# Memory attention and a maxout FFN on one core: output tiles in two pieces, and a new order of issue

## The chip, the cores and the metric

The kernel runs on one core of a Trainium2 chip. Its engines are TensorE (PE, matrix products into PSUM), VectorE (DVE), ScalarE (ACT) and GpSimd (POOL); SyncE (SP) issues transfers. Transfers run on 16 DMA engines. The metric is the device time of one execution in microseconds, the median of several runs; lower is better. PSUM has 8 banks of 512 fp32 columns on 128 partitions.

## The reference

Attention over 32 memory slots for 8 batches, 8 heads, 576 positions, head width 64, followed by an FFN whose hidden layer is the largest of three products:

```python
a = exp(phi - max_s phi);  a = a / (sum_s a + 1e-9)      # over positions s
k_m = einsum('bhsm,bhsd->bhmd', a, k)
v_m = einsum('bhsm,bhsd->bhmd', a, v)
attn = softmax(q @ k_m.T / 8) @ v_m                       # (b, h, s, d)
x = attn.transpose(0, 2, 1, 3).reshape(4608, 512)
h = max(max(x @ w1, x @ w2), x @ w3)                      # 512 -> 768
out = h @ w_out                                           # 768 -> 512, fp32
```

All inputs and the output are fp32 in HBM; the kernel's matrix products are in bf16.

## The kernel before, in words

**Staging.** q, k, v and phi come in whole batches. POOL issues these loads, and the weights; they convert to bf16 on the way, phi excepted. SP issues the first phi and the outputs. k and v of a batch lie in one of two buffers `kvo`; from batch 2 on POOL packs them into one of two buffers `kvr` (`pack`, L102), one copy for each of k and v, so that one product gives k_m, v_m and the softmax's denominators together. In batches 0 and 1 they are taken straight from `kvo`, in two parts. `ph` and `qq` have two buffers each. `wait_for` (L127) is a one-element copy on POOL that waits for half of k of batch 0, so that the loads issued behind it start later.

**One batch.** `att_exp` (ACT) gives e; `att_kv` (PE, L256) k_m and v_m; `att_kv_norm` (DVE) divides; `att_kv_t` transposes on PE and copies out. `att_q` (DVE) shuffles q; `att_score` (PE, L340) gives scores and ACT their exponentials; `att_t`, `att_sum`, `att_rec` (DVE), `att_mul` (POOL, L416) and `att_back` (DVE) make the probabilities `attn`, in two halves g = 0 and 1. Batch 0 takes its sums by PE instead (`ones_sum`, `ones_rec`, `ones_mul`).

**The FFN without the attention's last product.** v_m is multiplied into the weights: `fold` (PE, L447) gives wp = v_m times (w1-w3, w2-w3), and wp3 = v_m times (w3 times w_out), for 32 slots a head. `w_diff` (DVE) makes the differences in place; batch 0 folds w1, w2 and -w3 before they are made, in the column ranges of `FIRST`. `w3_t` and `w3_o` make w3 times w_out once. Then `ffn1` (PE, L473) is four products of 288 columns from attn and wp; w = 0 (even n) ends in a relu into h1, w = 1 (odd n) in a maximum with h1 on DVE into hT. So h - x w3 is what hT holds. `ffn2` (PE, L504 to L522) is one output tile of 128 rows: six products of hT with w_out and two of attn with wp3, summed in one PSUM bank, copied out, and stored by SP. Batches go in pairs of 1152 rows; tile t = 4 of an odd batch straddles the two batches of a pair (four half-width products). `ffn2_last` does the very last tile in two halves.

**The order.** Nothing reorders: each engine runs its instructions in the order in which a string of words at the end (L602 to L625) issues them. A word is a letter, a number and a batch: `F10@2` is `ffn1` n = 10 of batch 2. The letters are in `issue` (L568):

- L loads a batch (0 phi, 1 k, 2 v, 3 q), H half of k (even) or v (odd) of batch 0 (0, 1 the first half, 2, 3 the second); Y the weights (2 w3, 0 w1, 1 w2, 3 w_out); G the wait on POOL; r packs (0 k, 1 v); I identity and constants
- E exp of phi, B `att_kv`, N `att_kv_norm`, K `att_kv_t`, Q `att_q`, S `att_score`, a, s, c, m, X the softmax's steps, M and R the sums of batch 0, V `w_diff`
- D fold (3 is wp3), F `ffn1`, T `ffn2`, W and O the product of w3 and w_out, Z that many warm-up products of zeros

A "!" gives the copy out of PSUM to the other of ACT and DVE than the table `EVAC` says. A second string (`banks`, L145) gives the PSUM bank of each group in the order of issue; `one_bank` takes one, `two_banks` a pair. `fts` keeps the order in which a batch's hT tiles were made, and `ffn2` sums in this order.

Of the kernel before, what the change touches and what calls it, by code (L numbers as in the profile page):

```python
# [15 lines left out]
def kernel(  # L16
# [583 lines left out]


    for w in """  # L602
        E@0 H0@0 H2@0 L3@0 Z25@0 B0@0 I@0 N0@0 Z2@0 K0@0! Q0@0 Q1@0 Z9@0 S@0 Z2@0 M0@0 M1@0
        R0@0 Y2@0 G0@0 R1@0 W0@0 Y3@0 W1@0 W2@0 Z6@0 O1@0 H3@0 O3@0 O2@0 H1@0 X1@0 B1@0 X0@0 N1@0
        K1@0 O0@0 Y0@0 D1@0! D0@0! D3@0 F8@0 F10@0 F2@0 V0@0 F6@0 F0@0! Y1@0 D2@0 D4@0 F4@0
        L0@1 V1@0 F1@0 E@1 F3@0 L1@1 F5@0 F9@0 F7@0 L3@1 F11@0 B0@1 T3@0 N0@1 K0@1! L2@1 Q1@1
        L2@2 L1@2 Q0@1 L0@2 V2@0 T0@0! L3@2 S@1 T1@0 a0@1 s0@1 c0@1 m0@1 B1@1 N1@1 a1@1 L1@3
        K1@1 s1@1 D0@1 D1@1! D2@1 c1@1 m1@1 X0@1 L3@3 r1@2 X1@1 T2@0! L2@3 F6@1 F10@1 F7@1 F2@1
        F3@1 F4@1 F0@1 r0@2 E@2 F5@1 F1@1 F11@1 L0@3 L0@4 F8@1 L2@4 F9@1 B@2 D3@1 N@2 Q1@2
        T0@1! K@2 T2@1! r0@3 Q0@2 S@2 a0@2 a1@2 s1@2 c1@2 m1@2 T4@1! D1@2! s0@2 D2@2 c0@2 m0@2  # L610
        X1@2 D0@2 T3@1 Q0@3 L3@4 X0@2 Q1@3 T1@1 F0@2 F4@2 F8@2 F6@2 F9@2 E@3 F7@2 r1@3 F5@2
        F10@2 F1@2 B@3 L1@4 D3@2 N@3 L0@5 F2@2 F11@2 E@4 F3@2 L1@5 K@3 r1@4 L2@5 T2@2! S@3 T3@2
        a0@3 s0@3 c0@3 m0@3 D0@3 D2@3 a1@3 s1@3 c1@3 X0@3 D1@3! Q0@4 m1@3 T1@2 L3@5 L2@6 T0@2!
        X1@3 F10@3 r0@4 F2@3 F4@3 E@5 Q1@4 r0@5 F5@3 F3@3 L1@6 F8@3 B@4 N@4 D3@3 F9@3 F6@3
        F11@3 L0@6 K@4 F0@3 F7@3 F1@3 S@4 a0@4 T4@3! s0@4 a1@4 D0@4 c0@4 s1@4 r1@5 c1@4 D3@4
        m0@4 X0@4 Q0@5 T0@3! D1@4! D2@4 B@5 T3@3 m1@4 X1@4 L0@7 F10@4 Q1@5 N@5 F8@4 K@5 F6@4
        F9@4 S@5 F7@4 L3@6 F2@4 F4@4 a0@5 L1@7 a1@5 F0@4 s0@5 r1@6 F3@4 D0@5 r0@6 s1@5 c1@5 E@6
        D3@5 m1@5 c0@5 F1@4 T1@3 L2@7 F11@4 L3@7 E@7 F5@4 m0@5 B@6 D1@5! D2@5 X1@5 N@6 T2@3!
        X0@5 F6@5 F8@5 Q0@6 Q1@6 K@6 F4@5 F9@5 S@6 F7@5 r0@7 a0@6 F2@5 a1@6 s0@6 c0@6 F0@5
        F10@5 m0@6 F1@5 s1@6 c1@6 F11@5 F5@5 T0@4! F3@5 X0@6 T2@4! r1@7 D0@6 D1@6! Q0@7 B@7  # L620
        m1@6 N@7 X1@6 T2@5! K@7 T3@4 Q1@7 S@7 a0@7 F2@6 s0@7 a1@7 s1@7 c1@7 m1@7 c0@7 F4@6
        T4@5! D3@6 D2@7 D0@7! T0@5! D3@7 D2@6 X1@7 m0@7 D1@7! T1@4 X0@7 F6@7 F3@6 T1@5 F4@7
        F8@7 F0@7 F5@6 F10@6 F7@7 F9@7 F10@7 F5@7 F0@6 F11@7 F6@6 F1@7 F7@6 F2@7 F8@6 F11@6
        F9@6 F1@6 F3@7 T0@6! T0@7! T3@5 T2@7! T2@6! T1@6 T1@7 T3@6 T4@7! T3@7
    """.split():  # L625
# [32 lines left out]
```

## Time and profile before

| | |
|---|---|
| median of 3 runs | 165.57 us (165.14 to 166.01) |
| profiled execution, device time | 165.42 us |
| its span, first to last instruction | 163.7 us |
| last matmul starts its group at | 159.56 us |
| bytes moved by DMA | 31.77 MB, 194 GB/s over the span |
| output stores | 35 of 256 KB, two of 128 KB |

The span is what the profile's rows are measured in; the device time has 1.7 us around it. Lines of the timeline read: start, length, engine, line, operation, output<-input, number merged, and in brackets the idle time before it with what ended it. In the list of windows a row is the stretch, its length, then for PE, weight loads, DVE, ACT and POOL the busy time and the number of instructions, then the granted clock, the share of the DMA engines (over 1 where packets overlap) and GB/s. Lines of the chain are start, length and what ran. Ends of matmuls are modelled, so neighbouring groups overlap a little in these rows.

### The profile page before, as it was taken

What the parts mean: (1) busy time and instruction counts of PE and PEld (TensorE: products, weight loads), DVE (VectorE), ACT (ScalarE), POOL (GpSimd) and SP (SyncE); (2) the same over time, 40 slices, a digit from 0 to 9 for tenths busy, and PEclk for the clock granted to TensorE, in tenths of its full rate; (3) what the DMA queues carried; (4) which work ended last, traced back from release to release, by engine and by line L of the source; (5) the groups of instructions that cost most, each with busy time, mean ns of one, the idle gap of its engine ahead of it and who ended that gap; (6) DMA issues with size and microseconds to landing.
All of it is one profiled execution on the core that took longest, in us unless ns stands there. A gap on an engine that the chain in (4) does not pass through costs nothing.

```text
span 163.7 us, 4819 instructions
## 1 busy us (share of the span) xinstructions
PE 153.0 (93%) x2060; PEld 85.5 (52%) x2080; DVE 90.4 (55%) x181; ACT 100.5 (61%) x151; POOL 69.7 (43%) x72
## 2 busy tenths in 40 slices
PE   7987798999898999999999999999999999999990
PEld 2442444664376436753673575576553467744450
DVE  2023703898837765759399759879749228810000
ACT  4205335935496488778885989994658976323320
POOL 7275215100698276838939976755403200000000
PEclk9999999999999999999999999999999999999999
DMA  5999999999999999999999999997313230014333
GB/s 155 156 207 200 197 210 213 277 208 208 259 307 241 209 257 364 277 216 286 258 265 206 233 351 266 175 235 157 130 70 125 73 128 0 0 68 180 141 128 130
DMA packets 21974, 31.77 MB, mean 194 GB/s; under 512 B 1216, under 2 KB 16576, under 8 KB 21952
## 3 DMA queue, kind: packets, MB, share of 16 engines
q0 software_dynamic: 16080, 21.43, 68.7%
q1 hardware_dynamic: 5728, 9.90, 17.2%
q8 instruction: 16, 0.26, 0.6%
q10 hardware_dynamic: 144, 0.13, 0.2%
q14 instruction: 6, 0.05, 0.1%
HBM read 39.32 MB, written 9.44 MB: 298 GB/s over the span
## 4 chain that ended last, share of the span: by engine, by line
PE 65%; DMA 28%; POOL 2%; issue 2%; ACT 1%; POOLq 0%; ACTq 0%
PE psum L504 25%; PE psum L473 22%; DMA ph<-in_phi_dram 15%; DMA w_sb<-in_moe_w_dram 9%; PE psum L513 7%; DMA kvo<-in_k_dram 4%; PE psum L447 4%; PE psum L256 3%; PE psum L340 1%; POOL kvo L97 1%; PE psum L522 1%; PE psum L545 1%; ACT e L236 1%; PE psum L305 1%; POOL wo_sb L123 0%
## 5 line engine op out<-in xcount | busy, mean ns | idle before, releaser
L504 PE MATMUL psum<-wo_sb,hT 128*128 128x512 bf16 x193 | 49.7, 380 | 1.4 <-issue 0.6
L473 PE MATMUL psum<-attn,wp 128*128 128x288 bf16 x384 | 50.5, 286 | 0.1
L486 DVE TENSOR_TENSOR hT<-psum,h 128x576 bf16<-128x576 f32 x48 | 34.2, 749 | 18.2 <-PE psum L473 12.0
L473 PEld LDWEIGHTS <-wp 128*128 128x128 bf16 x384 | 36.7, 98 | 13.2 <-issue 1.9
L179 ACT COPY ot<-psum 128x512 f32<-128x512 f32 x35 | 20.7, 591 | 32.1 <-PE psum L513 25.2
L504 PEld LDWEIGHTS <-hT 128*128 128x128 bf16 x210 | 19.2, 98 | 24.1 <-issue 4.3
L103 POOL COPY kvr<-kvo 128x2304 bf16<-128x2304 bf16 x12 | 25.4, 2114 | 14.3 <-DMA kvo<-in_k_dram 7.9
L179 ACT CAST wp<-psum 128x1024 bf16<-128x1024 f32 (+1 forms) x31 | 29.3, 996 | 3.0 <-PE psum L447 2.1
L177 ACT ACTIVATE h<-psum 128x576 bf16<-128x576 f32 x47 | 28.4, 659 | 3.2 <-PE psum L473 3.1
L416 POOL TENSOR_TENSOR t<-t,sm 128x576 bf16<-128x576 bf16 x14 | 16.1, 1157 | 25.2 <-DVE sm L411 25.1
L513 PE MATMUL psum<-wp,attn 128*128 128x512 bf16 x62 | 18.4, 379 | 0.0
L166 PE MATMUL psum<-warm 128*128 128x512 bf16 x42 | 12.4, 450 | 1.4 <-DVE warm L135 1.2
L320 DVE STREAM_TRANSPOSE qT<-qq 128x576 f32<-128x576 f32 x16 | 11.7, 747 | 1.5 <-DMA qq<-in_q_dram 1.5
L349 ACT ACTIVATE e<-psum 128x576 bf16<-128x576 f32 x16 | 9.6, 652 | 3.8 <-PE psum L340 3.8
L236 ACT ACTIVATE e<-ph 128x1152 bf16<-128x1152 f32 (+1 forms) x9 | 9.6, 1065 | 2.6 <-DMA ph<-in_phi_dram 2.4
L402 DVE TENSOR_REDUCE sm<-t 128x18 f32<-128x576 bf16 x14 | 10.3, 738 | 0.2
L97 POOL DMA_DIRECT2D kvo<-in_v_dram x9 | 6.7, 747 | 7.2 <-PE psum L256 4.1
L513 PEld LDWEIGHTS <-attn 128*128 128x128 bf16 x62 | 6.1, 98 | 7.1
L394 DVE STREAM_TRANSPOSE t<-e 128x288 f32<-128x288 f32 x14 | 6.3, 464 | 6.2 <-ACT e L349 6.1
L562 DVE COPY ot<-psum 128x256 f32<-128x256 f32 x1 | 0.4, 425 | 15.4 <-PE psum L553 15.4
L256 PEld LDWEIGHTS <-e 64*32 64x32 bf16 x720 | 6.9, 90 | 3.4 <-issue 2.0
L166 PEld LDWEIGHTS <-warm 128*128 128x128 bf16 x44 | 4.6, 111 | 7.4 <-issue 3.5
(58 smaller groups left out, 116.4 us busy)
## 6 DMA issues: line engine op xcount, KB each, us to landing
out_dram<-ot SPq DMA_DIRECT2D x35, 256.0 KB, 5.5
qq<-in_q_dram POOLq DMA_DIRECT2D x8, 576.0 KB, 12.6
ph<-in_phi_dram POOLq DMA_DIRECT2D x7, 576.0 KB, 15.1
kvo<-in_k_dram POOLq DMA_DIRECT2D x7, 576.0 KB, 13.9
kvo<-in_v_dram POOLq DMA_DIRECT2D x7, 576.0 KB, 16.6
w_sb<-in_moe_w_dram POOLq DMA_DIRECT2D x3, 768.0 KB, 15.0
wo_sb<-in_moe_w_out_dram POOLq DMA_DIRECT2D x1, 768.0 KB, 10.7
ph<-in_phi_dram SPq DMA_DIRECT2D x2, 288.0 KB, 2.9
```

Of the source, the lines that this page charges most:

```text
L103: nc.gpsimd.tensor_copy(out=kvrs[b % 2][:, :, :, D * i : D * (i + 1)], in_=kvos[b % 2][:, 1 - i])
L166: nc.tensor.matmul(po[:, 0:BANK], lhsT=warm[:, 0:P], rhs=warm, start=True, stop=True)
L177: nc.scalar.activation(out=out_, in_=in_, func=AF.Relu)
L179: nc.scalar.copy(out=out_, in_=in_)
L236: nc.scalar.activation(out=s["e"][:, js], in_=loaded[b]["ph"][:, js], func=AF.Exp)
L256: nc.tensor.matmul(kvp[M * j : M * (j + 1), a, 0:nd], lhsT=s["e"][r, j, c, :], rhs={None: lambda: kvr[r, j, c, 0:nd], 0: lambda: k_and_one ...
L320: nc.vector.transpose(out=s["qT"][:, j].rearrange("p j c r e -> p (j c r e)").bitcast(FP32), in_=loaded[b]["q"][:, j].rearrange("p j c d - ...
L416: nc.gpsimd.tensor_tensor(out=t, in0=t, in1=s["sm", g].unsqueeze(2).to_broadcast([P, S // HP, R, 2]), op=ALU.mult,)
L473: nc.tensor.matmul(acc[:, h, 0:SH], lhsT=wps[b][:, g, w * DF + ft * P : w * DF + (ft + 1) * P], rhs=attn[:, g, c0 : c0 + SH], start=(g == ...
L486: nc.vector.tensor_tensor(out=hT[:, ft, (b % 2) * S : (b % 2 + 1) * S].rearrange("p (h n) -> p h n", h=2), in0=a, in1=s["h1", ft], op=ALU.max,
L504: nc.tensor.matmul(po, lhsT=hT[:, fc, c0 : c0 + P], rhs=wo_sb[:, fc, :], start=(n == 0), stop=False,)
L513: nc.tensor.matmul(po, lhsT=attn[:, g, c0 : c0 + P], rhs=wp3s[b][:, g, :], start=False, stop=(g == NG - 1),)
```

## The change

- A new word P is `ffn2_head`: the first three of the six hT products of an output tile, into a bank of its own that is held. The word T of the same tile later takes this bank and does the remaining three and the two with wp3. Tiles without a P are whole as before.
- Tile t = 4 does its products with wp3 first and those with hT after.
- `w_diff` works on the ranges of `FIRST`, one instruction a word: V0, V1, V2 and V4 in place of V0, V1 (two instructions) and V2.
- The strings of order and banks are new from start to end: q of batch 0 is loaded first, then the second half of k and the first; the identity is made behind POOL's wait; phi and q of batch 3 are loaded ahead of v and k of batch 3; packs, folds, `ffn1` and tiles stand elsewhere; more copies out of PSUM have a "!".

```diff
--- before.py
+++ after.py
@@ -41,6 +41,7 @@
     FT = DF // P
     SH = S // 2
     BANK = 512
+    HEAD = 3
 
     const = ctx.enter_context(tc.tile_pool(name="const", bufs=1))
     inp = ctx.enter_context(tc.tile_pool(name="inp", bufs=2))
@@ -145,9 +146,9 @@
     banks = iter(
         "".join(
             """
-            00224460026701101401264026402640264026452063420643064206420642064562074206742064
-            20642064201640264102640264026402640264072406247026402640264024602406520462046204
-            62704267402640264124602416420642064206420642067676767670
+            30303012464064726746246024026420642064744074644020426024604260427012442067406420
+            46240642014264621046620642064206425602062672020724042064024602402656056042064202
+            4062452654260620162404204624026420462406240340607336334
             """.split()
         )
     )
@@ -214,16 +215,13 @@
 
     def w_diff(n):
 
-        c, end = n * BANK, (n + 1) * BANK
-        while c < end:
-            e = min(end, (c // DF + 1) * DF)
-            nc.vector.tensor_tensor(
-                out=w12[:, :, c:e],
-                in0=w12[:, :, c:e],
-                in1=w_sb[:, :, 2, c % DF : c % DF + e - c],
-                op=ALU.subtract,
-            )
-            c = e
+        lo, end = FIRST[n]
+        nc.vector.tensor_tensor(
+            out=w12[:, :, lo:end],
+            in0=w12[:, :, lo:end],
+            in1=w_sb[:, :, 2, lo % DF : lo % DF + end - lo],
+            op=ALU.subtract,
+        )
 
     ln = const.tile([P, S], FP32, name="ln")
     ONES = {(0, 0), (0, 1)}
@@ -492,15 +490,15 @@
 
     osts = {}
 
-    def ffn2(b, t, swap):
-
-
-        hT, attn = hts[b // 2], attns[b // 2]
-        c0 = S - HP if t == 4 else (b % 2) * (S + HP) + t * P
-        if b == B - 1 and t == 3:
-            return ffn2_last(b, c0)
-        po = one_bank()
-        for n, fc in enumerate(fts[b]):
+    heads = {}
+
+    def ffn2_head(b, t):
+
+        hT = hts[b // 2]
+        c0 = (b % 2) * (S + HP) + t * P
+        po = heads[b, t] = one_bank()
+        for n in range(HEAD):
+            fc = fts[b][n]
             nc.tensor.matmul(
                 po,
                 lhsT=hT[:, fc, c0 : c0 + P],
@@ -508,8 +506,38 @@
                 start=(n == 0),
                 stop=False,
             )
-        for g in range(NG):
-            if t < 4:
+
+    def ffn2(b, t, swap):
+
+
+        hT, attn = hts[b // 2], attns[b // 2]
+        c0 = S - HP if t == 4 else (b % 2) * (S + HP) + t * P
+        if b == B - 1 and t == 3:
+            return ffn2_last(b, c0)
+        po = heads[b, t] if (b, t) in heads else one_bank()
+
+        if t == 4:
+            for g in range(NG):
+                for u in range(2):
+                    nc.tensor.matmul(
+                        po[HP * u : HP * (u + 1)],
+                        lhsT=attn[:, g, c0 + HP * u : c0 + HP * (u + 1)],
+                        rhs=wp3s[b - 1 + u][:, g, :],
+                        start=(g == 0),
+                        stop=False,
+                        tile_position=(0, HP * u),
+                    )
+        for n in range(HEAD if (b, t) in heads else 0, FT):
+            fc = fts[b][n]
+            nc.tensor.matmul(
+                po,
+                lhsT=hT[:, fc, c0 : c0 + P],
+                rhs=wo_sb[:, fc, :],
+                start=(n == 0 and t < 4),
+                stop=(n == FT - 1 and t == 4),
+            )
+        if t < 4:
+            for g in range(NG):
                 nc.tensor.matmul(
                     po,
                     lhsT=attn[:, g, c0 : c0 + P],
@@ -517,16 +545,6 @@
                     start=False,
                     stop=(g == NG - 1),
                 )
-            else:
-                for u in range(2):
-                    nc.tensor.matmul(
-                        po[HP * u : HP * (u + 1)],
-                        lhsT=attn[:, g, c0 + HP * u : c0 + HP * (u + 1)],
-                        rhs=wp3s[b - 1 + u][:, g, :],
-                        start=False,
-                        stop=(g == NG - 1),
-                        tile_position=(0, HP * u),
-                    )
         ot = opool.tile([P, DM], FP32, name="ot")
         r0 = (b // 2) * 2 * S + c0
         rows = out[r0 : r0 + P, :]
@@ -590,6 +608,7 @@
             "R": lambda: ones_rec(b, i),
             "D": lambda: fold(b, i, swap),
             "F": lambda: ffn1(b, i, swap),
+            "P": lambda: ffn2_head(b, i),
             "T": lambda: ffn2(b, i, swap),
             "W": lambda: w3_t(i, swap),
             "O": lambda: w3_o(i, swap),
@@ -600,28 +619,30 @@
 
 
     for w in """
-        E@0 H0@0 H2@0 L3@0 Z25@0 B0@0 I@0 N0@0 Z2@0 K0@0! Q0@0 Q1@0 Z9@0 S@0 Z2@0 M0@0 M1@0
-        R0@0 Y2@0 G0@0 R1@0 W0@0 Y3@0 W1@0 W2@0 Z6@0 O1@0 H3@0 O3@0 O2@0 H1@0 X1@0 B1@0 X0@0 N1@0
-        K1@0 O0@0 Y0@0 D1@0! D0@0! D3@0 F8@0 F10@0 F2@0 V0@0 F6@0 F0@0! Y1@0 D2@0 D4@0 F4@0
-        L0@1 V1@0 F1@0 E@1 F3@0 L1@1 F5@0 F9@0 F7@0 L3@1 F11@0 B0@1 T3@0 N0@1 K0@1! L2@1 Q1@1
-        L2@2 L1@2 Q0@1 L0@2 V2@0 T0@0! L3@2 S@1 T1@0 a0@1 s0@1 c0@1 m0@1 B1@1 N1@1 a1@1 L1@3
-        K1@1 s1@1 D0@1 D1@1! D2@1 c1@1 m1@1 X0@1 L3@3 r1@2 X1@1 T2@0! L2@3 F6@1 F10@1 F7@1 F2@1
-        F3@1 F4@1 F0@1 r0@2 E@2 F5@1 F1@1 F11@1 L0@3 L0@4 F8@1 L2@4 F9@1 B@2 D3@1 N@2 Q1@2
-        T0@1! K@2 T2@1! r0@3 Q0@2 S@2 a0@2 a1@2 s1@2 c1@2 m1@2 T4@1! D1@2! s0@2 D2@2 c0@2 m0@2
-        X1@2 D0@2 T3@1 Q0@3 L3@4 X0@2 Q1@3 T1@1 F0@2 F4@2 F8@2 F6@2 F9@2 E@3 F7@2 r1@3 F5@2
-        F10@2 F1@2 B@3 L1@4 D3@2 N@3 L0@5 F2@2 F11@2 E@4 F3@2 L1@5 K@3 r1@4 L2@5 T2@2! S@3 T3@2
-        a0@3 s0@3 c0@3 m0@3 D0@3 D2@3 a1@3 s1@3 c1@3 X0@3 D1@3! Q0@4 m1@3 T1@2 L3@5 L2@6 T0@2!
-        X1@3 F10@3 r0@4 F2@3 F4@3 E@5 Q1@4 r0@5 F5@3 F3@3 L1@6 F8@3 B@4 N@4 D3@3 F9@3 F6@3
-        F11@3 L0@6 K@4 F0@3 F7@3 F1@3 S@4 a0@4 T4@3! s0@4 a1@4 D0@4 c0@4 s1@4 r1@5 c1@4 D3@4
-        m0@4 X0@4 Q0@5 T0@3! D1@4! D2@4 B@5 T3@3 m1@4 X1@4 L0@7 F10@4 Q1@5 N@5 F8@4 K@5 F6@4
-        F9@4 S@5 F7@4 L3@6 F2@4 F4@4 a0@5 L1@7 a1@5 F0@4 s0@5 r1@6 F3@4 D0@5 r0@6 s1@5 c1@5 E@6
-        D3@5 m1@5 c0@5 F1@4 T1@3 L2@7 F11@4 L3@7 E@7 F5@4 m0@5 B@6 D1@5! D2@5 X1@5 N@6 T2@3!
-        X0@5 F6@5 F8@5 Q0@6 Q1@6 K@6 F4@5 F9@5 S@6 F7@5 r0@7 a0@6 F2@5 a1@6 s0@6 c0@6 F0@5
-        F10@5 m0@6 F1@5 s1@6 c1@6 F11@5 F5@5 T0@4! F3@5 X0@6 T2@4! r1@7 D0@6 D1@6! Q0@7 B@7
-        m1@6 N@7 X1@6 T2@5! K@7 T3@4 Q1@7 S@7 a0@7 F2@6 s0@7 a1@7 s1@7 c1@7 m1@7 c0@7 F4@6
-        T4@5! D3@6 D2@7 D0@7! T0@5! D3@7 D2@6 X1@7 m0@7 D1@7! T1@4 X0@7 F6@7 F3@6 T1@5 F4@7
-        F8@7 F0@7 F5@6 F10@6 F7@7 F9@7 F10@7 F5@7 F0@6 F11@7 F6@6 F1@7 F7@6 F2@7 F8@6 F11@6
-        F9@6 F1@6 F3@7 T0@6! T0@7! T3@5 T2@7! T2@6! T1@6 T1@7 T3@6 T4@7! T3@7
+        L3@0 H2@0 E@0 H0@0 Z36@0 B0@0 Y2@0 G0@0 Y3@0 I@0 Q1@0 N0@0 Q0@0 Z3@0 K0@0! Z6@0 W2@0
+        W1@0 W0@0 S@0 M0@0 Z3@0 O0@0! R0@0 H3@0 M1@0 O3@0 H1@0 B1@0 R1@0 N1@0 X1@0 X0@0 O2@0
+        K1@0! Y0@0 O1@0 D1@0! V1@0 D0@0! D3@0 F8@0! Y1@0 V0@0 F10@0 F0@0 F2@0 F6@0! D2@0 L0@1
+        L1@1 D4@0 V4@0 F4@0 F3@0 F1@0 F9@0 L3@1 L2@1 L2@2 F5@0 L1@2 F11@0 E@1 F7@0 L0@2 L3@2
+        L0@3 P3@0 B0@1 N0@1 Q0@1 T1@0 K0@1! Q1@1 T3@0! S@1 V2@0 a0@1 P2@0 s0@1 B1@1 N1@1 c0@1
+        P0@0 L3@3 a1@1 m0@1 s1@1 K1@1! c1@1 X0@1 T2@0! D0@1! D1@1! m1@1 D2@1 L2@3 r1@2 X1@1
+        T0@0! F0@1 F10@1! F8@1 F2@1 r0@2 F1@1 F11@1 F4@1 F6@1! F9@1 E@2 F5@1 F3@1 P2@1 F7@1 B@2
+        D3@1 N@2 P0@1 P3@1 K@2! L1@3 T3@1 Q0@2 Q1@2 S@2 a1@2 T2@1! E@3 L2@4 a0@2 L0@4 L1@4 s0@2
+        c0@2 s1@2 c1@2 m0@2 Q1@3 m1@2 L3@4 r1@3 X0@2 r0@3 T0@1! D1@2 L2@5 X1@2 r1@4 D0@2 D2@2
+        T4@1! T1@1! F6@2 F2@2! F7@2 Q0@3 F4@2 F10@2 F3@2 F8@2 F5@2 F9@2 F0@2 F11@2 B@3 N@3 L0@5
+        D3@2 E@4 F1@2 P2@2 K@3 P1@2 S@3 a0@3 T1@2! T2@2! a1@3 s0@3 s1@3 c1@3 L1@5 r0@4 D1@3!
+        c0@3 D3@3 Q0@4 m0@3 D2@3 P3@2 P0@2 B@4 D0@3 L3@5 Q1@4 X0@3 m1@3 T3@2! X1@3 r1@5 T0@2!
+        F6@3 F2@3 F0@3 N@4 F8@3 L0@6 F1@3 F10@3 F7@3 E@5 K@4 F9@3 F3@3 F4@3 F11@3 P0@3 F5@3
+        P1@3 L1@6 S@4 r0@5 L3@6 T4@3! a0@4 s0@4 L2@6 B@5 D1@4! a1@4 s1@4 N@5 c1@4 D2@4 Q0@5
+        T1@3 m1@4 Q1@5 c0@4 m0@4 K@5 X1@4 P2@3 L0@7 T0@3! S@5 L1@7 X0@4 a0@5 T2@3! r0@6 F8@4
+        s0@5 L3@7 a1@5 F10@4 P3@3 s1@5 c1@5 c0@5 D3@4! L2@7 D0@4 D1@5! m0@5 T3@3 F9@4 F4@4!
+        m1@5 F0@4 F5@4 X0@5 F2@4 F6@4 X1@5 F3@4 E@6 F7@4 r1@6 F1@4 F10@5 r0@7 F11@4 P2@4 Q0@6
+        B@6 D0@5! D2@5 T0@4! N@6 F6@5! E@7 Q1@6 Q1@7 F0@5 K@6 T2@4! F2@5! F8@5 F7@5 F3@5 F9@5
+        P3@4 F1@5 F4@5 Q0@7 r1@7 F11@5 T3@4! S@6 B@7 N@7 D3@5 F5@5 P2@5 K@7! T2@5! a0@6 S@7
+        P1@4 a0@7 P3@5 a1@7 D1@7! s0@6 s0@7 D2@7 c0@6 D3@7 a1@6 s1@6 m0@6 s1@7 T3@5 c0@7 T1@4!
+        X0@6 c1@7 m0@7 X0@7 c1@6 D3@6! m1@7 m1@6 D0@7 T1@5 T0@5 D1@6! X1@6 D0@6! X1@7 D2@6
+        T4@5! F4@7 F2@6 F4@6! F6@6 F7@6 F0@7 F3@6 F5@7 F8@7 F5@6 F8@6 F1@7 F6@7! F10@6 F10@7
+        F9@7 F11@6 F11@7 F0@6! P0@7 F9@6 F2@7 P2@6 F1@6 F3@7 P1@7 T2@6! F7@7 T4@7! T2@7 T1@7
+        T1@6 T0@6! T3@6! T0@7! T3@7
     """.split():
         n, b = w.rstrip("!").split("@")
         issue(int(b), n, w.endswith("!"))
```

## The prediction

> **What bounds the kernel now.** I read the page's slices first, then the windows, TensorE's own timeline, and last POOL's timeline, because POOL issues every load after the first.
>
> ```profile
> span 163.7 us, 4819 instructions
> PE 153.0 (93%) x2060; PEld 85.5 (52%) x2080; DVE 90.4 (55%) x181; ACT 100.5 (61%) x151; POOL 69.7 (43%) x72
> PE   7987798999898999999999999999999999999990
> PEclk9999999999999999999999999999999999999999
> DMA  5999999999999999999999999997313230014333
> ```
>
> Two rows are full: TensorE (PE) to the end, the DMA engines until about 113 us (slice 27; a slice is 4.1 us). The clock is full everywhere. The windows show how little PE idles once the first weights are in:
>
> ```profile
> 26.70:35.00 8.30, 8.22 (x152) 5.57 (x153) 6.69 (x9) 7.26 (x11) 1.50 (x2) 1.00 1.17 245
> 35.00:43.30 8.30, 7.45 (x202) 3.50 (x180) 7.24 (x16) 3.13 (x6) 1.03 (x1) 1.00 1.20 221
> 43.30:52.30 9.00, 8.54 (x87) 5.68 (x90) 5.29 (x9) 7.42 (x11) 8.34 (x8) 1.00 1.15 279
> 60.00:70.00 10.00, 10.00 (x148) 6.54 (x141) 7.07 (x16) 8.66 (x13) 7.29 (x7) 1.00 1.11 318
> ```
>
> The second pair of columns is PE's busy time: idle is 0.08, 0.85, 0.46 and 0.00 us. From 26.7 us to the last matmul all windows together leave 2.7 us idle, half of it in pieces of 0.05 to 0.2 us with no visible releaser. A reordering can win back about 1.3 us (0.85 + 0.46) and no more, unless the first 26.7 us shrink. These are set by loads, as the chain says (start, length):
>
> ```profile
> 11.61 15.00 DMA w_sb<-in_moe_w_dram
> 27.17 23.86 DMA ph<-in_phi_dram
> ```
>
> w1 lands at 26.6 us and the first fold starts at 26.70; phi of batch 2 lands at 51.0. So what counts is when later loads land. POOL tells it where it packs k and v into kvr and had to wait (brackets):
>
> ```profile
> 57.34 2.11 POOL L103 COPY kvr<-kvo 128x2304 bf16<-128x2304 bf16 x1 [3.32 <-DMA kvo<-in_k_dram]
> 64.87 2.10 POOL L103 COPY kvr<-kvo 128x2304 bf16<-128x2304 bf16 x1 [1.43 <-DMA kvo<-in_v_dram]
> 72.34 2.11 POOL L103 COPY kvr<-kvo 128x2304 bf16<-128x2304 bf16 x1 [2.74 <-DMA kvo<-in_v_dram]
> 84.55 2.11 POOL L103 COPY kvr<-kvo 128x2304 bf16<-128x2304 bf16 x1 [2.92 <-DMA kvo<-in_k_dram]
> 97.92 2.11 POOL L103 COPY kvr<-kvo 128x2304 bf16<-128x2304 bf16 x1 [1.12 <-DMA kvo<-in_k_dram]
> ```
>
> They are k3, v3, v4, k5 and k6 (letter and batch). Call q, k or v of a batch one unit, phi half. POOL issued, after phi 2: q2, k3, q3, v3, phi 3, phi 4, v4, q4, k4, phi 5, k5, v5, q5, v6, k6. That puts 2, 4, 6, 9.5 and 13.5 units behind 51.0 us at 57.3, 64.8, 72.3, 84.5 and 97.9: 3.47 us a unit, between 3.13 and 3.75 in any stretch. The loads come one behind the other.
>
> **Head: q first.** The same bytes precede w1 in both orders (phi, q, k, w3, wo, v), so w1 stays at 26.6. q, which landed at 12.1, changes places with k (9.2): B0@0 moves from 9.16 to about 12.1. Eleven more warm-up matmuls (Z36) at 0.22 us fill that wait; the fold cannot start sooner anyway. The gate on POOL now waits for the first-issued k half, about 10.7, and wo's issue (0.8), the identity (0.5) and the kvr memsets (0.4) stand behind it, which gives ident by 12.2, before K0 asks at about 14. v and w1 are issued about 3 us later, at 13 to 16, but w3 occupies the engines until 16.2. Then W (1.5) after w3, S 17.8, softmax pieces, and O0 (1.3) on wo at 20.1, M1 (0.25), O3 (1.3), B1 (0.75), O2 (1.3), K1 (0.1), O1 (1.3): 26.4. D1@0 starts at 26.7 as now. Head: 0, with -0.5 to +0.5 for q landing in one piece or POOL's later issues. SP issues only the first phi and the outputs, both unmoved relative to what it waits for: 0.
>
> **Amount of work.** w_diff splits its range elsewhere, with the same columns and four instructions (0.68 to 1.2 us each, DVE). A tile T is eight matmuls (1.73 us), now often P (three, 0.65) and the rest (1.08); none is added, and the t=4 tile only swaps the order inside. From D1@0 to the end I add, for each order, F 0.49 (9.80/20), T 1.73, T4 1.84, B 0.73, S 0.42, K 0.17, D 0.28: 129.1 us both times. The trace needs 133.25 for it. Seven casts change sides: evacuations on DVE grow by 5 folds (1.22), 10 relu (0.76) and 9 output copies (about 0.65), less 4 kvt copies (0.36): about +18 us on DVE (90 to about 108, 66% of the span), and about as much less on ACT. Cost 0 while DVE has room; its chains are priced below.
>
> **Start of batches 0 to 2.** Gains: K1@1 follows B1@1 at once today (PE waits 0.43 for kvn, then 0.32 for kvt); P0@0 and T2@0's rest now stand there: -0.75. P2@1 is done ahead of B@2, where PE now waits 0.41: -0.4. Losses, hand-ordered on DVE: P3@0 needs hT of F9@0, behind V4 (1.2) and F6's relu, +0.3; B1@1 moves to 40.2 but v1 follows q1 (37.5) by a unit, 41.0, +0.8; X1@1 stands behind D0@1's cast (1.22), F0@1's second half +0.5; S@2 waits for Q1@2, +0.25. Together +0.7, ends -1.15 (only the gains) and +1.85 (no gain). I take B@2 at 52.3 to 53.1.
>
> **The place that decides: B@4.** From B@2 to B@4 there are now 18 F, eight T and one T4 with the small parts, 29.3 us by the sum and 29.8 in the trace (52.27 to 82.04). After the change there are 12 F, one T, five rests, six P and T4: 23.5. So 5.2 us of work (5.3 in real time) is pushed behind B@4, which PE reaches at 52.3 to 53.1 + 23.9 = 76.2 to 77.0. B@4 needs both packs, thus k4. The new POOL order after phi 2 is q2, phi 3, q3, v3, k3, v4, phi 4, k4: 7 units instead of 8. By the rows (6 units 72.3, 9.5 units 84.5) k4 lands at 75.8. r1@4 (v4, 70.4) and two load issues (0.75 each) are through by 74.0, then r0@4 takes 2.1: 77.9. B@4 starts at 78.0, whatever was won or lost before. That is 4.0 us earlier than today with 5.2 us more left to do: 81.7 against 76.5 by the sum, and the trace needs 77.9 for the latter, so 83.2. Last matmul 78.0 + 83.2 = 161.2, now 159.95: **+1.2**. Ends by unit: 3.13 gives k4 72.9 and no wait, 3.75 gives 77.3 and +2.7.
>
> Queued behind r0@4 on POOL are m0@3, the issue of q5 (0.8) and m1@3 (1.15 each): done at 81.0. X1@3 (0.48) ends at 81.6, and F6@3, which PE reaches at 81.0, needs it for its second half: **+0.25** (0 to 0.6).
>
> The other packs have room: k3 (4.5 units, 66.7) makes B@3 possible at 68.9, PE is there at 69.1 to 69.4; k5 (10.5 units, 87.9) 90.0 against 91.5; v6 (15 units, 103) 105.2 against 107; v7 about 117.7 against 119. K@5 and S@5 lie on one DVE stretch: a 0.5, s 0.75, a, s, N 1.0, two Q (0.75 each), two c (0.27), kvt copy 0.36 from 90.3, ending at 96.1, where PE arrives at 95.8: **+0.4** (0 to 0.8). The tail stays (T3@7 last, two halves, out by 1.7 us).
>
> **Sum.** 1.2 + 0.25 + 0.4 = 1.85. The profiled execution took 165.42 us (span 163.7 and 1.7 around it), 0.15 below the median 165.57 of the three runs. 165.42 + 1.85 = 167.27; I say **167.2**.
>
> One rule of the Trainium skill speaks against this wait ("DMA: Bandwidth & Descriptors", section Bandwidth): about 358 GB/s is a core's share of HBM. A unit reads 1.18 MB, an estimate of 3.3 us by that figure, k4 at 74.1 and the pack done at 76.2, so no wait at B@4 and a time as in the rival below. The trace's 3.47 contains output stores on the same engines, which go on after the change, so I keep it.
>
> **Rivals.** (1) The loads are in time: at the fastest stretch, 3.13 us a unit, the pack ends at 75.1, B@4 follows PE at 76.2 to 77.0; today's order has the same work left at 82.04 - 5.3 = 76.8. That is -0.6 to +0.2, with S@5's wait 165.2 to 166.0. For it: one stretch ran so. Against: three later stretches at 3.5 to 3.75. (2) Faster, the other side: the heads do fill both waits and DVE keeps up, -1.15 and nothing back: 164.3. It decides if k4 lands before 73.5 and B1@1 does not wait for v1. Against: v1 cannot precede q1. (3) DVE becomes the bound: with 18 us more, every softmax chain of batches 1 to 7 waits another 0.3 to 0.5 us on PE: 2 to 3.5 us more, 169.3 to 170.8. For it: DVE's 7.24 of 8.30 us in the second window above. Against: the distance on PE from S to the first F of its batch stays or grows (5.5 to 5.5, 6.6 to 7.0, 6.5 to 7.8, 7.5 to 8.1 us).
>
> **Chances.** Forecast 0.58, rival 1 0.22, rival 2 0.10, rival 3 0.10. The forecast's own range is 166.3 to 169.0. Half a per cent, 0.83 us, is what can be told from no change. Forecast counts as slower but for 0.02, rival 3 too, rival 1 as same but for 0.02 faster: faster 0.12, same 0.22, slower 0.66. Range 165.0 to 169.4.
>
> **What would show it.** Right: POOL's r0@4 waits for k until about 76 and B@4 follows its end at 78 with a PE gap of about 1 us; B0@0 at 12, D1@0 at 26.7; m0@3 directly behind the pack; P groups without gaps. Wrong: r0@4 without a wait, D1@0 off 26.7 by over 0.5, or the gap in batches 5 to 7.

## The result, and the profile after

| | before | after |
|---|---|---|
| median of 6 runs each, side by side | 165.11 us (164.68 to 166.01) | 167.49 us (166.17 to 168.74) |
| ratio, with its 95% interval | | 1.0135 (1.0091 to 1.0178) |
| profiled execution, its span | 165.42 us, 163.7 | 168.51 us, 166.7 |

The change makes the kernel slower, by 2.4 us at the median. The six runs after lie in two groups, around 166.6 and 168.5, and the profiled one is of the upper group: its trace shows 3.0 us more span, of which about 1 us is not in every run.

The page of the kernel after, first the totals, then the slices of 4.2 us:

```profile
span 166.7 us, 4820 instructions
PE 153.2 (92%) x2060; PEld 86.5 (52%) x2084; DVE 107.5 (64%) x202; ACT 87.4 (52%) x130; POOL 69.6 (42%) x72
PE   7956899799999999999999999899999999999991
PEclk9997899999999999999999999999999999999997
DMA  5999999999999999999999999997011530002443
```

TensorE does the same work (153.2 us against 153.0) in a longer span, so what is lost is waiting. DVE is busy 17.1 us more (about 18 was worked out) and ACT 13.1 us less (about as much was); DVE is not full. New are the 5 and 6 early in PE's row, a granted clock of 0.7 and 0.8 in the fourth and fifth slice, the 7 in the eighth, and an 8 at 104 to 108 us. The windows place it (columns as before: stretch, length, PE, weight loads, DVE, ACT, POOL, clock, DMA share, GB/s):

```profile
10.00:20.00 10.00, 7.05 (x142) 3.94 (x142) 3.43 (x7) 0.37 (x1) 6.71 (x13) 0.83 1.17 192
26.70:35.00 8.30, 7.10 (x108) 4.11 (x107) 6.84 (x8) 6.16 (x11) 2.10 (x3) 1.00 1.16 245
35.00:43.30 8.30, 8.04 (x154) 4.66 (x154) 7.61 (x14) 3.45 (x7) 1.49 (x2) 1.00 1.21 209
43.30:52.30 9.00, 8.90 (x144) 5.38 (x145) 7.08 (x15) 6.10 (x10) 7.01 (x5) 1.00 1.14 292
100.00:110.00 10.00, 8.88 (x164) 6.01 (x145) 8.21 (x15) 6.10 (x9) 6.64 (x6) 1.00 1.15 280
```

From 35.0 to 52.3 us PE is busy 16.94 us, where it was busy 15.99: the waits that the divided tiles could fill are filled. The losses are ahead of that (7.10 of 8.30 us where it was 8.22) and in the last window (8.88, where it was 9.89; the row of the kernel before):

```profile
100.00:110.00 10.00, 9.89 (x182) 6.13 (x177) 7.92 (x18) 9.62 (x13) 5.99 (x6) 1.00 1.17 211
```

TensorE's timeline names them:

```profile
13.45 0.80 PE L254 MATMUL psum<-kvo,e 64*32 64x128 bf16 x72 [2.65 <-DMA kvo<-in_k_dram]
17.92 1.67 PE L192 MATMUL psum<-ident,w_sb 128*128 128x128 bf16 x24
28.34 0.30 PE L445 MATMUL psum<-w_sb,kvt 64*32 64x256 bf16 x8
33.27 0.30 PE L445 MATMUL psum<-w_sb,kvt 64*32 64x256 bf16 x8 [1.04 <-DMA w_sb<-in_moe_w_dram]
54.64 0.80 PE L254 MATMUL psum<-kvr,e 64*32 64x129 bf16 x72
76.79 0.41 PE L445 MATMUL psum<-w_sb,kvt 64*32 64x512 bf16 x8 [0.26 <-DVE ot L184]
78.96 0.80 PE L254 MATMUL psum<-kvr,e 64*32 64x129 bf16 x72
108.59 0.80 PE L254 MATMUL psum<-kvr,e 64*32 64x129 bf16 x72 [0.91 <-POOL kvr L104]
115.22 1.51 PE L471 MATMUL psum<-attn,wp 128*128 128x288 bf16 x11 [0.22 <-DVE kvt L184]
```

They are B0@0, W, D1@0, D2@0, B@2, D1@3, B@4, B@6 and F7@5. B0@0 waits for k until 13.45, and the first fold starts at 28.34, 1.64 us later than before; the second waits another 1.04 us for w2. The two folds in the kernel before:

```profile
26.70 0.30 PE L447 MATMUL psum<-w_sb,kvt 64*32 64x256 bf16 x8
30.49 0.30 PE L447 MATMUL psum<-w_sb,kvt 64*32 64x256 bf16 x8
```

The first one starts when w1 is there. The trace has the landing time of every load, and w1 lands at 28.30 after and at 26.61 before; in this and the eleven other profiles of this document D1@0 starts within 0.1 us behind the landing of w1. w2 lands at 33.23, 4.93 us behind w1; in ten of the eleven others it is 3.8 us, so 1.1 us of the delay of D2@0 belongs to this one execution.

B@4 has no wait, and the wait for a pack stands at B@6. POOL's timeline shows the packs of k3, k4, k5 and v6, and m0@3:

```profile
68.05 2.11 POOL L104 COPY kvr<-kvo 128x2304 bf16<-128x2304 bf16 x1 [0.83 <-DMA kvo<-in_k_dram]
76.58 2.11 POOL L104 COPY kvr<-kvo 128x2304 bf16<-128x2304 bf16 x1 [0.63 <-DMA kvo<-in_k_dram]
78.92 1.15 POOL L414 TENSOR_TENSOR t<-t,sm 128x576 bf16<-128x576 bf16 x1 [0.24 <-DVE sm L409]
89.45 2.11 POOL L104 COPY kvr<-kvo 128x2304 bf16<-128x2304 bf16 x1 [1.99 <-DMA kvo<-in_k_dram]
106.44 2.10 POOL L104 COPY kvr<-kvo 128x2304 bf16<-128x2304 bf16 x1 [1.89 <-DMA kvo<-in_v_dram]
```

Every one of these packs waits for its load, and only that of v6, which ends at 108.54, is later than TensorE.

To see where the lag arises I set the start of each word against the time at which the kernel before has the same amount of work left, by the prediction's sums (F 0.49 us, T 1.73 and so on). For B@2 that is 52.9, as a little less is left there than at before's B@2.

| start of | after | before, same work left | lag |
|---|---|---|---|
| D1@0 | 28.34 | 26.70 | +1.6 |
| D2@0 | 33.27 | 30.49 | +2.8 |
| B@2 | 54.64 | 52.9 | +1.7 |
| B@4 | 78.96 | 76.8 | +2.15 |
| B@6 | 108.59 | 105.9 | +2.7 |
| end of the last matmul | 163.0 | 159.95 | +3.1 |

So in this execution the head loses 2.8 us, batches 0 to 2 win 1.1 back, and 1.4 us are lost from batch 3 on, where the largest single wait is the 0.9 at B@6.

### The profile page after: what moved, and what is told of

Read it like the earlier page. It is cut to its first block, busy times and chain, and to the rows that moved or that the text cites. A ratio compares the mean times of both kernels' runs of the same rounds, so it can differ in the third digit from the quotient of the medians.

```text
span 166.7 us, 4820 instructions
## 1 busy us (share of the span) xinstructions
PE 153.2 (92%) x2060; PEld 86.5 (52%) x2084; DVE 107.5 (64%) x202; ACT 87.4 (52%) x130; POOL 69.6 (42%) x72
## 5 line engine op out<-in xcount | busy, mean ns | idle before, releaser
L532 PE MATMUL psum<-wo_sb,hT 128*128 128x512 bf16 x135 | 34.6, 380 | 1.1 <-issue 1.0
L178 ACT ACTIVATE h<-psum 128x576 bf16<-128x576 f32 x37 | 23.0, 652 | 14.9 <-PE psum L471 14.3
L180 ACT CAST wp<-psum 128x1024 bf16<-128x1024 f32 (+1 forms) x26 | 24.4, 984 | 9.8 <-PE psum L445 7.5
L180 ACT COPY ot<-psum 128x512 f32<-128x512 f32 x26 | 15.3, 590 | 22.8 <-PE psum L541 19.3
L532 PEld LDWEIGHTS <-hT 128*128 128x128 bf16 x144 | 12.6, 98 | 17.1 <-issue 4.9
L502 PE MATMUL psum<-wo_sb,hT 128*128 128x512 bf16 x56 | 16.5, 380 | 0.7 <-issue 0.3
L167 PE MATMUL psum<-warm 128*128 128x512 bf16 x46 | 13.8, 456 | 1.4 <-DVE warm L136 1.2
L184 DVE COPY ot<-psum 128x512 f32<-128x512 f32 x9 | 6.1, 680 | 9.4 <-PE psum L541 6.0
L182 DVE TENSOR_SCALAR h<-psum 128x576 bf16<-128x576 f32 x11 | 8.3, 753 | 3.5 <-PE psum L471 3.5
L111 POOL DMA_DIRECT2D qq<-in_q_dram x8 | 6.3, 788 | 9.1 <-DMA w_sb<-in_moe_w_dram 4.2
```

What stands on the lines that cost most here:

```text
L167: nc.tensor.matmul(po[:, 0:BANK], lhsT=warm[:, 0:P], rhs=warm, start=True, stop=True)
L178: nc.scalar.activation(out=out_, in_=in_, func=AF.Relu)
L180: nc.scalar.copy(out=out_, in_=in_)
L502: nc.tensor.matmul(po, lhsT=hT[:, fc, c0 : c0 + P], rhs=wo_sb[:, fc, :], start=(n == 0), stop=False,)
L532: nc.tensor.matmul(po, lhsT=hT[:, fc, c0 : c0 + P], rhs=wo_sb[:, fc, :], start=(n == 0 and t < 4), stop=(n == FT - 1 and t == 4),)
```

## The experiments

Ratios are to the kernel before, measured beside each. L, H and E are loads of a batch, of half of k or v, and the exponentials of phi.

**The old loads in the new order.** Everything as after, but the first loads in the order phi, k, k, q, with the warm-up cut to match.

```diff
-        L3@0 H2@0 E@0 H0@0 Z36@0 B0@0 Y2@0 G0@0 Y3@0 I@0 Q1@0 N0@0 Q0@0 Z3@0 K0@0! Z6@0 W2@0
+        E@0 H0@0 H2@0 L3@0 Z25@0 B0@0 I@0 Y2@0 G0@0 Y3@0 N0@0 Q1@0 Q0@0 Z3@0 K0@0! Z20@0 W2@0
```

> The changed kernel with the head's loads in the old order (phi, k first half, k second half, q; identity ahead of POOL's wait) and warm-ups to suit. Theory A (the loss is made in the head: w2 lands 2.8 us later when q is first, of which 1.2 us is won back by batch 2, and 0.9 us is lost at B@6): D2@0 is back at 30.5, the end comes 2.8 us earlier, about 165 us beside 165.1 for the kernel before. Theory B (the prediction's: k of batch 4 and its pack hold B@4 at 78 us whatever the head does): D2@0 is back at 30.5 too, PE now stands 1 to 2 us at B@4, and the time is 166.5 to 167.

Measured: 165.99 us, ratio 1.0059 (1.0032 to 1.0086). That is 1.5 us less than after by the medians, and 1.25 by the ratios, whose intervals leave about 0.4 to 2.1: by the middle values q first is half of the loss or more. The first fold starts at 27.14 (w1 lands at 27.10) and B@4 at 76.76 with no idle time before it. But TensorE now stands twice before a pack; B@5 and B@6 in its timeline, and the packs of k4, k5 and v6 in POOL's:

```profile
90.78 0.80 PE L254 MATMUL psum<-kvr,e 64*32 64x129 bf16 x72 [0.78 <-POOL kvr L104]
106.85 0.80 PE L254 MATMUL psum<-kvr,e 64*32 64x129 bf16 x72 [0.53 <-POOL kvr L104]
```

```profile
74.38 2.11 POOL L104 COPY kvr<-kvo 128x2304 bf16<-128x2304 bf16 x1 [0.63 <-DMA kvo<-in_k_dram]
88.62 2.11 POOL L104 COPY kvr<-kvo 128x2304 bf16<-128x2304 bf16 x1 [2.02 <-DMA kvo<-in_k_dram]
104.69 2.11 POOL L104 COPY kvr<-kvo 128x2304 bf16<-128x2304 bf16 x1 [1.89 <-DMA kvo<-in_v_dram]
```

k4 is early enough. From there on a load takes longer than the 3.47 us that I had: 8 units from k4 to v6 in 30.31 us, 3.79 each (in after 29.86, or 3.73). Each of these packs waited for its load, so they give landing times.

**q first in the old order.** The kernel before, with only its first loads changed, and the warm-ups to suit.

```diff
-        E@0 H0@0 H2@0 L3@0 Z25@0 B0@0 I@0 N0@0 Z2@0 K0@0! Q0@0 Q1@0 Z9@0 S@0 Z2@0 M0@0 M1@0
+        L3@0 H2@0 E@0 H0@0 Z36@0 B0@0 I@0 N0@0 Z2@0 K0@0! Q0@0 Q1@0 Z2@0 S@0 Z2@0 M0@0 M1@0
```

> The kernel before with nothing but the head's loads in the new order (q, second half of k, first half) and warm-ups to suit. Theory A: w2 lands late, D2@0 starts near 33 instead of 30.5, nothing later in this order gives it back: 167 to 168 us. Theory B (head costs nothing, as predicted, -0.5 to +0.5): 164.6 to 165.6 us.

Measured: 166.97 us, ratio 1.0110 (1.0069 to 1.0151), 1.9 us slower than the kernel before beside it. Nothing else is changed, so q first by itself costs about as much as in the new order. B0@0 and the first fold in TensorE's timeline:

```profile
13.03 0.80 PE L256 MATMUL psum<-kvo,e 64*32 64x128 bf16 x72 [1.44 <-DMA kvo<-in_k_dram]
...
27.54 0.30 PE L447 MATMUL psum<-w_sb,kvt 64*32 64x256 bf16 x8
```

Before, q was the last of q and k to land, at 12.1 us; with q first the last one, k, starts B0@0 0.9 us later than that here and 1.35 later in after. w1 lands at 27.49.

**Is it the clock?** In after PE idles 2.65 us ahead of B0@0, and from 15 to 18 us the granted clock is at half. Ten more warm-up products close most of the gap.

```diff
-        L3@0 H2@0 E@0 H0@0 Z36@0 B0@0 Y2@0 G0@0 Y3@0 I@0 Q1@0 N0@0 Q0@0 Z3@0 K0@0! Z6@0 W2@0
+        L3@0 H2@0 E@0 H0@0 Z46@0 B0@0 Y2@0 G0@0 Y3@0 I@0 Q1@0 N0@0 Q0@0 Z3@0 K0@0! Z6@0 W2@0
```

> The changed kernel with 46 instead of 36 warm-up products, which fill the 2.65 us in which PE waited for k and after which its clock fell to half for 3.2 us. Rival C (the fallen clock is the loss): 1 to 1.5 us faster than the changed kernel. Theory A (w2's landing at 33.2 ends the wait at D2@0, PE had 1.0 us of slack there): no change, within 0.3 us of it.

Measured: 167.60 us, ratio 1.0139 (1.0096 to 1.0182), the same as after. The clock stays at 1.0 through the head and W starts at 17.36 instead of 17.92; even so:

```profile
13.73 0.80 PE L254 MATMUL psum<-kvo,e 64*32 64x128 bf16 x72 [1.06 <-DMA kvo<-in_k_dram]
...
28.51 0.30 PE L445 MATMUL psum<-w_sb,kvt 64*32 64x256 bf16 x8
```

The clock is not the cause: the first fold comes no earlier, as w1 lands at 28.47 here.

**Is it the gate?** POOL's wait for half of k ends at 11.89 in after (9.27 before), and w_out, v, w1 and w2 are issued behind it. The word is taken out.

```diff
-        L3@0 H2@0 E@0 H0@0 Z36@0 B0@0 Y2@0 G0@0 Y3@0 I@0 Q1@0 N0@0 Q0@0 Z3@0 K0@0! Z6@0 W2@0
+        L3@0 H2@0 E@0 H0@0 Z36@0 B0@0 Y2@0 Y3@0 I@0 Q1@0 N0@0 Q0@0 Z3@0 K0@0! Z6@0 W2@0
```

> The changed kernel, q first, without POOL's wait for the half of k, so that w_out, v, w1 and w2 are issued at once. In the changed kernel the wait opens at 11.9 instead of 9.3 us, only w3 is then in flight, and the DMA rate dips to 124 GB/s at 14 to 15 us. Theory A1 (the late gate starves the engines): D2@0 starts 1 us or more earlier than 33.3, the time falls by 1 to 1.5 us to about 166.3. Theory A2 (q and k together land 1.4 us later, whatever is behind them): no change, 167.5, or slower, since w_out then competes with k.

Measured: 167.33 us, ratio 1.0115 (1.0074 to 1.0155); no difference from after that could be told. In its profile B0@0 starts at 12.90 and the first fold at 27.50, so the head of this one execution is better, but the median does not follow. Taking the late gate away brings nothing that can be told.

**Without the split.** All three-product heads empty; each T does its eight products where its second part stood.

```diff
-    HEAD = 3
+    HEAD = 0
```

> The changed kernel with the heads empty: P still takes its bank, the tile's eight matmuls all run at T. Theory A and the prediction's step on the start of batches 0 to 2: the split fills the wait for K1@1 and part of the way to B@2, so without it 0.7 to 1.2 us more than the changed kernel. Rival: the waits are filled by whatever stands there and the split is worth nothing: the changed kernel's 167.5 within 0.5 us.

Measured: 176.14 us, ratio 1.0672 (1.0633 to 1.0711): 8.6 us more than after, where I expected about one. The trace shows why that was far too little: waits in nearly every batch, the largest of which, behind the head, in the list of TensorE's waits (total, times, longest) are:

```profile
PE psum L303 <- DVE kvn L278: 1.4, 2, 0.8
PE psum L471 <- DVE hT L484: 1.0, 2, 0.7
PE psum L303 <- DVE kvn L288: 0.9, 4, 0.3
PE psum L254 <- ACT wp L180: 0.9, 1, 0.9
PE psum L445 <- ACT e L347: 0.8, 1, 0.8
```

All its waits after 35 us add up to 7.8 us, against 1.4 in after. Twelve of the 22 P stand right ahead of a K, an S or a B, which need DVE, ACT or a load first, and without the P that wait is bare. So in this order the split is needed; what this does not say is that the order with the split beats the old order without.

**Are the loads behind the waits at B@5 and B@6?** With the old loads kept, only the first half of q is loaded from batch 4 on. The second half of the heads of batches 4 to 7 is computed from the first half's q, so that part of the output is left out; every instruction stays, and only half the bytes of four loads go.

```diff
+        h = halves[0] if b >= 4 else slice(0, NP)
         nc.gpsimd.dma_start(
-            out=qq.rearrange("p j c d -> p j (c d)"), in_=by_pair(q, b)
+            out=qq.rearrange("p j c d -> p j (c d)")[:, h], in_=by_pair(q, b)[:, h]
         )
...
-            in_=loaded[b]["q"][:, j].rearrange("p j c d -> p (j c d)").bitcast(FP32),
+            in_=loaded[b]["q"][:, halves[0] if b >= 4 else j].rearrange("p j c d -> p (j c d)").bitcast(FP32),
```

> e1_old_loads with only the first half of q loaded from batch 4 on; the second half of the heads is computed from the first half's q, so that part of the output is left out. 0.5 unit less is loaded before k5 (1.7 us at 3.5 us a unit) and 1.5 units less before v6 (5 us). If the loads cause the waits at B@5 and B@6: both go, 1.3 us less than e1_old_loads, about 164.7. Rival (the packs are late for POOL's own order): the waits stay, 166.0.

Measured: 164.86 us, ratio 0.9986 (0.9962 to 1.001), 1.1 us less than with whole loads. No pack is waited for any more. Some of what is left in TensorE's list of waits:

```profile
PE psum L533 <- issue: 1.0, 6, 0.2
PE psum L446 <- DMA w_sb<-in_moe_w_dram: 0.6, 1, 0.6
PE psum L446 <- DVE ot L185: 0.5, 1, 0.5
PE psum L503 <- issue: 0.3, 2, 0.2
```

So the loads are the cause of the second part. The run also tells the worth of the rest: with the old head and no late pack, the new order only equals the old one within the interval. Of the gain of 1 us in batches 0 to 2, D1@3 gives 0.5 back here (the third row).

The rows with "issue" look like idle time and are not. They are eight pauses of 0.16 to 0.22 us, each ahead of a group that has one product too few: the profile lost some records of products. TensorE's products and weight loads of the whole tiles and the second parts, from the page of this run, and the products in the run with the old loads and whole q, which has the same order:

```profile
L533 PE MATMUL psum<-wo_sb,hT 128*128 128x512 bf16 x135 | 34.6, 380 | 1.2 <-issue 1.0
L533 PEld LDWEIGHTS <-hT 128*128 128x128 bf16 x144 | 12.6, 98 | 17.2 <-issue 5.1
```

```profile
L532 PE MATMUL psum<-wo_sb,hT 128*128 128x512 bf16 x144 | 36.7, 380 | 0.0
```

Where all 144 products are recorded, no such pause is there. The kernel before has four pauses of the same kind (193 products for 210 weight loads), so its true idle time is 0.6 us less than the prediction read.

**Moving work ahead of the waits.** Can B@5 and B@6 simply come later? With the old loads, one tile goes ahead of B@5, one ahead of K@5, and a tile and a fold ahead of B@6.

```diff
+ T1@3 ahead of B@5;  T0@3 ahead of K@5;  T0@4 and D0@5 ahead of B@6;  K@6! behind T2@4
```

> e1_old_loads with B@5 and B@6 moved 1.1 and 1.7 us further back on PE (T1@3 ahead of B@5, T0@3 ahead of K@5, T0@4 and D0@5 ahead of B@6, K@6 after T2@4 and copied by ACT). In e1_old_loads PE waits 0.78 us at B@5 and 0.53 at B@6 for packs that follow k5 and v6, and 0.22 for the copy of K@6 on DVE. If late loads are what is left of the loss: these waits go, 1.3 to 1.5 us less, about 164.6. Rival (the wait only moves: the loads or DVE stop PE a little later, at S@5, S@6 or B@7): less than 0.4 us gained, about 165.8.

Measured: 166.69 us, ratio 1.0086 (1.0067 to 1.0106); no gain. B@5 and B@6 no longer wait, but the work is now missing behind them, and the chains on DVE come bare:

```profile
94.49 0.48 PE L338 MATMUL psum<-qT,kvt 32*32 32x288 bf16 x32 [0.50 <-DVE kvt L184]
...
109.86 1.14 PE L471 MATMUL psum<-attn,wp 128*128 128x288 bf16 x8 [1.10 <-DVE kvn L288]
```

**The same, with the scores of batch 0 ahead of W and T1@2 copied by ACT.**

```diff
- K0@0! Z20@0 W2@0 W1@0 W0@0 S@0 M0@0 Z3@0 O0@0!
+ K0@0! Z9@0 S@0 Z4@0 M0@0 R0@0 M1@0 R1@0 Z6@0 W2@0 W1@0 W0@0 Z3@0 O0@0!
...
- T1@2!
+ T1@2
```

> e5_b56_later with the scores and sums of batch 0 ahead of W in the head, as in the kernel before, and T1@2 copied by ACT, so that D1@3 does not wait 0.28 us for DVE. If D1@0 is held by PE's own chain in e1_old_loads (27.14 instead of 26.70): 0.2 to 0.5 us less than e5_b56_later, about 164.3, below the kernel before. Rival (w1 and w2 land when they land): equal to it within 0.2 us.

Measured: 166.17 us, ratio 1.0064 (1.004 to 1.0088), no difference from the last version that could be told. The first fold waits for w1:

```profile
26.59 0.30 PE L445 MATMUL psum<-w_sb,kvt 64*32 64x256 bf16 x8 [0.25 <-DMA w_sb<-in_moe_w_dram]
```

In the last version it started at 26.21, with w1 landing at 26.17, so the moved scores bring it no earlier. D1@3 waits 0.51 us for ACT where it waited 0.43 for DVE. The wait of 1.10 us is unchanged.

**v of batch 6 loaded ahead of q of batch 6.** Old loads, scores ahead of W, K@6's copy by ACT, and one load moved.

```diff
- L3@6 T4@3! a0@4 s0@4 L2@6
+ L2@6 L3@6 T4@3! a0@4 s0@4
```

> e1_old_loads with v6 loaded ahead of q6 (3.5 us earlier for the pack that B@6 waits for), K@6 copied by ACT, and the scores of batch 0 ahead of W as in e6_all. If the loads are what is left: the waits of 0.53 us at B@6 and 0.22 us behind K@6 go, B@5's 0.78 stays: 0.7 to 1.0 us less than e1_old_loads, about 165.1, equal to the kernel before. Rival (the wait moves on, as it did in e5_b56_later): 166.0.

Measured: 165.67 us, ratio 1.0029 (1.0007 to 1.0051), the least of the versions that compute everything, still not below the kernel before. B@6 waits no more. In its profile, of an execution of 167.64 us, B@5, which the move does not touch, still waits 1.03 us for its pack, and B@7 now waits 0.33.

**Two split tiles in the old order.** The order and first loads of the kernel before, with T1@0 and T0@1 in two parts, put where its trace shows waits of 0.43 and 0.41 us. The code is that of after, so t = 4 also has its products in the new order.

```diff
- T1@0 a0@1 s0@1 c0@1 m0@1 B1@1 N1@1 a1@1 L1@3 K1@1 ... F9@1 B@2 D3@1
+ P1@0 a0@1 s0@1 c0@1 m0@1 B1@1 N1@1 a1@1 L1@3 T1@0 K1@1 ... F9@1 P0@1 B@2 D3@1
```

> The order of before, with before's first loads, and only two tiles in two pieces: three products of T1@0 stay where the tile stood and the other five go between B1@1 and K1@1; three products of T0@1 go ahead of B@2. Both places are waits of TensorE in the trace of before: 0.43 us for kvn ahead of K1@1 and 0.41 us for E@2's exponentials ahead of B@2. Theory A (split tiles are worth the waits that they fill, and the head and the loads are what the change lost): 0.84 us less, some 164.3 us, ratio 0.995; PE shows neither wait. Theory B (what is won in batches 1 and 2 is given back at the next thing that comes at a fixed time, a pack or a load): both waits gone, new ones behind them, 165.0 to 165.4, ratio 0.999 to 1.002.

Measured: 166.16 us, ratio 1.0064 (1.0042 to 1.0085): slower than either theory had it. The profile is of the longest of the six executions, 167.40 us. B0@1, P0@1 and the last two products of T0@1 in TensorE's timeline:

```profile
36.31 0.80 PE L254 MATMUL psum<-kvo,e 64*32 64x128 bf16 x72 [1.21 <-DVE hT L484]
...
53.39 0.81 PE L502 MATMUL psum<-wo_sb,hT 128*128 128x512 bf16 x2 [0.29 <-DVE hT L484]
...
56.26 0.59 PE L541 MATMUL psum<-wp,attn 128*128 128x512 bf16 x2 [0.35 <-ACT wp L180]
```

The two filled waits come back as two others: P0@1 waits 0.29 us for the third hT tile, and the rest of T0@1 needs wp of D3@1 sooner than it is copied (0.35). The wait of 1.21 us at B0@1 lies ahead of any tile that was divided. The list names a DVE instruction, but by the landing times it is the load of k1: k1 lands at 36.17 here and at 34.64 before, and B0@1 starts 0.14 and 0.16 us behind it; q1 too is 1.1 us later (its first shuffle starts at 38.68, not 37.58). That is this one execution. Why the median of this version lies a full microsecond above before is not settled; the order of the products of t = 4 was not tried alone.

## Why the prediction was right, and where it was not

The time, 167.2, and the sign were right, and that is in part luck: none of the three terms of the sum of 1.85 us was paid at the place where it was put, and a head priced at nothing made up for it. The mechanism behind the largest term, a pack that waits for its load, was right. By the medians, the 2.4 us are: 1.5 for the head's loads (after less the version with old loads), 1.1 for late packs (that version less the one with half of q), and -0.2 for everything else. By the intervals the first two are known to within 0.6 to 0.9 us each, so which is the larger is open.

- **Head, 0: wrong.** It cost 1.5 us, 1.9 in the old order. The step that failed is "the same bytes precede w1 in both orders, so w1 stays at 26.6", with k taken to land where q had, at 12.1. Same bytes did not mean same time: the last of q and k lands at 12.8 to 13.6 in the five profiles with q first, and at 11.4 to 12.6 in the seven with the old loads. w1, and with it D1@0, follows: 27.5 to 28.5 in the five, 26.1 to 27.7 in the seven. On average the five are 1.1 us later at the last of q and k, 0.5 at w3, 1.2 at w_out and 1.25 at w1: w_out lands 3.7 to 3.9 us behind w3 with the old loads and 4.3 to 4.9 with q first. The bound of +0.5 was too tight by 1 us.
- **Start of batches 0 to 2, +0.7 within -1.15 to +1.85: the gain end came.** The lag falls by 1.1 us between D2@0 and B@2. None of the losses for DVE or v1 was there: B1@1 waited 0.05 us, P3@0 not at all. The late head is not the reason: reckoned in the same way, the lag falls by 1.0 to 1.1 us there in seven of the eight profiles that have this order and the split, with early heads and late ones (by 0.7 in the eighth), and without the split it grows by 0.45.
- **B@4, +1.2: right mechanism, wrong place.** k4 landed at 76.5 against 75.8 worked out, but the late head brought PE to B@4 at 78.96, after the pack. With the head repaired the pack ended at 76.49 and PE came at 76.76. The price was paid at B@6, and with the old loads at B@5 too, where I had said that k5 (87.9) and v6 (103) leave room: they landed at 89.4 and 106.4, and at 88.6 and 104.6 with the old loads. The term that was too small is the 3.47 us a unit; from k4 to v6 it was 3.73. I had 3.75 as an end of the range, but asked what it does at B@4 alone.
- **DVE, +0.25 at F6@3 and +0.4 at S@5: about the right size, at other places.** m0@3 did stand directly behind the pack, but F6@3 did not wait, as PE was late. D1@3 waits 0.26 us for an output copy that now goes through DVE. F7@5 waits 0.22 us for the copy of K@6, which DVE made before too; it now stands on DVE behind a shuffle of q7, which waits for its load until 114.15. The third rival, 2 us or more on DVE, did not come.
- **Idle time:** of the 2.7 us from which the prediction started, 0.6 are lost records and no idle time. No term of the sum used them.
- **The page's rule.** By the 358 GB/s of the Trainium skill ("DMA: Bandwidth & Descriptors", Bandwidth) a unit takes an estimated 3.3 us, k4 lands at 74.1 and B@4 does not wait. B@4 indeed waited in neither order of the loads, but not because of that figure. With the old loads the exponentials of batch 2 start at 50.02 without waiting for phi, in ACT's timeline:

```profile
50.02 1.16 ACT L234 ACTIVATE e<-ph 128x1152 bf16<-128x1152 f32 x1
```

phi had landed by then, so the 7 units to k4 (74.38) took at least 3.48 us each, and the 8 after them 3.79. The traces stay above the 3.3 us in both stretches, and by more in the later one. Nor is the rate a ceiling here: in after, the 15 units from phi 2 (52.28) to v6 (106.39) and the 14 stores beside them are 21.4 MB in 54.1 us, an estimate of 395 GB/s.

The first rival (loads in time, 165.2 to 166.0) is what the version with the old loads gives, by another way: 165.99, with B@4 as that rival had it and the later packs not. Of the signs named for a wrong forecast two were there, D1@0 off by more than 0.5 us and a gap in batches 5 to 7, though the time was right. A time that fits is no proof of its terms.

## What to carry to other kernels

Where loads form one queue, a changed order of the first few is not neutral because the bytes are: give their landing a term of its own, as large as the spread of landing times in the trace. Work out every later meeting of a load and its reader with the slowest unit the trace shows, not only the first meeting; repairing one wait sends the reader to the next. And a part of a tile fills a wait only until its own inputs are asked for earlier: the two filled waits of 0.84 us brought back 0.64 us at their new places. Before you count a short pause with no releaser as idle time, compare the numbers of products and weight loads on the line: a lost record looks the same.

## What the runs showed of the hardware

- Loads issued in the same order land at times that differ by 1 us and more between executions: w1 between 26.1 and 27.7 us in seven profiles with the old first loads, and between 27.5 and 28.5 in five with q first; q1, with the loads of before, is there for its shuffle at 37.58 and 38.68. Why everything lands later with q first was not found; taking the gate away or keeping the clock up brought nothing back.
- After 2.65 us without work TensorE's granted clock was at half from 15 to 18 us (0.83 over the window from 10 to 20). Gaps of 2.08 and 1.44 us at the same place in other versions had no such consequence. It held W to 17.92, where w3 had landed at 17.02, but the first fold followed the landing of w1 (28.30), so the halved clock did not show in the time.
- Between the loads of k4 and v6 a load of 1.18 MB takes 3.7 to 3.8 us; from k3 to k4 it took 3.4 (2.5 units in 8.53 us). Output stores are denser there: in after, 5 were issued in the 7 units from phi 2 to k4 and 9 in the 8 units from k4 to v6, and in the kernel before 3 in the 4.5 units from k4 to v6, at 3.3 us a unit. The two go together; no run changes the stores alone.
- A profile can lose records of products: 135 of 144 on one line with half of q, none with the old loads, and each pause of 0.16 us without a releaser is the place of one.
